# Moving the token stage's tiles under the next stage's first operand, and dropping seven lead steps, in a fused attention forward and backward kernel

## The chip, the cores and the metric

The kernel runs on one core of a Trainium2 chip, as one program. The metric is the device time of a run in microseconds (us); lower is better. The engines are TensorE (PE in the profile, with its weight loads as PEld), VectorE (DVE), ScalarE (ACT), GpSimd (POOL) and SyncE (SP), which here only issues transfers; DMA engines move the data.

## The reference

The reference is the output of a gated mixture of two attention branches, and its gradients with respect to eleven inputs. There are 2048 tokens with 576 channels. Branch A has 32 query heads of 18 channels that share one key and one value head. Branch B goes through the tokens in 64 segments of 32, with 8 memory rows that each segment hands to the next, and has 32 heads of 128 channels.

```
g = sigmoid((x * gate_w).sum(-1))
a = softmax(q k^T / sqrt(18)) v  @ wo          # branch A, all tokens
for s in range(64):                            # branch B
    h = concat([mem, x_s]);  q, k, v = h Wq, h Wk, h Wv
    o = softmax(mask(q k^T / sqrt(128))) v  @ Wo
    mem, out_s = o[:8], o[8:]
out = g * a + (1 - g) * b;   grads = vjp(grad_out)
```

## The kernel before, in words

The program is a row of stages on one core.

1. Preparation and projections, up to about 500 us.
2. The forward weave: the recurrent chain of branch B's segments, with the first pass of branch A between its steps.
3. The token stage, `b_bulk`, about 2040 to 2673 us. It goes through the tokens in 32 chunks (a tile of 128 tokens, half of the heads) of four groups each: scores, softmax, outputs and their gradients for branch B's tokens. The work is a pipeline of short steps over 137 ticks: a group's queries are turned at its own tick and its last step, `st_Qx`, which reads the chunk's keys, comes nine ticks later.
4. The backward weave: the recurrent chain backwards, 64 segments of 14 steps (`b_chain_bwd`), with the second pass of branch A (`a_pass2`, called the sweep: 1024 steps in all) between its steps. `weave` makes one sweep step per chain step. Before the chain it makes `lead` steps without a chain: each of these runs a sweep step, then `early_bwd(i)`, which issues loads, then, from step PRE on, a piece of `lead_dw`, eleven matmuls of two weight gradients of branch A.
5. `b_post`, then `b_dw`: the weight gradients of branch B, with the rest of the sweep, one step each time that the matmuls have streamed WCOLS columns; then `a_final`.

The order on every engine is that of the program, written out by hand. A tile's place in on-chip memory follows from the order of the pools and of the first allocations in them. A stage's tiles overlie those of the stage before it, and a first write waits for the last use of the tiles that lie there. [...]

Names that the steps below touch, with the lines of the profile:

- `x_q`, `x_dO`, `x_k` (L758): 128 x 16 x 128 in bf16, 4,096 B a partition, four buffers of each, rotated by chunk; they are called deep. `x_v` has three buffers, the memory keys and values `x_kmT` and `x_vmT` (L749) two each. `x_kmB` and `x_vmB` (L752), two each of 4,096 B, are masked copies in the pool `xw`, written into their diagonal blocks and zeroed once.
- `x_po<-x_kmB,x_DT` and `x_po<-x_k,x_DT`: the matmuls of `st_Qm` and `st_Qx` (L87 is the line of the helper that makes every matmul). `dqx_dram<-x_dq` (L788): the store of a chunk's query gradients, issued by `flush`; from tick 129 on, `flush` issues on ScalarE's queue.
- `WT` (three tiles of 128 x 32 x 576, 36,864 B a partition): first the operands of `lead_dw`, WT[0] with dq and x (L681, L682), WT[1] with o and da (L684, L686), then the transposed weights of the chain (L1064), two heads of each group of eight at a time, so four loads a tile. `WoT` (L673) is another weight of the chain.
- `r_pj<-WT` and `r_x<-WT`: the matmuls of `lead_dw` (in the chain, `r_pj<-WT,r_dT` are the matmuls `heads` with the weights). `r_kvo` (L712) carries results of `lead_dw` to the output.
- `b_QS` (L2023): the sweep's operand for four steps, loaded by SyncE in the weave and by ScalarE in `b_dw`; `b_S`, `b_dP`, `b_acc`: its matmuls; `b_E` (L2037) the exponential on ScalarE, `b_dS` (L2088) the product on VectorE.

Of the kernel before, what the change touches and what calls it, by code (L numbers as in the profile page):

```python
# [12 lines left out]
BF16 = mybir.dt.bfloat16  # L13
# [3 lines left out]
P = 128  # L17
# [18 lines left out]
KR = 9  # L36
KVT = 11
KV4 = 9
SWEEP = 932
QSW = 800  # L40
WCOLS = 13824
PRE = 7
RIDE = 24


# [6 lines left out]
class Kern:  # L52
# [245 lines left out]
    def weave(self, chain, sweep, lead, extra=(), early=None, pre=None):  # L298
        steps = itertools.count()

        def step():
            i = next(steps)
            next(sweep, None)
            if early is not None:
                early(i)
            if pre is not None and i >= PRE:
                next(pre, None)
# [369 lines left out]
    def early_bwd(self, i):  # L677
        ld = self.nc.sync.dma_start
        v = lambda d: d[:, 0:D].rearrange("(p n) d -> p n d", p=P)
        if i == 0:  # L680
            ld(self.WT[0][:, 16:32, :], v(self.dqtok_dram))  # L681
            ld(self.WT[0][:, 0:16, :], v(self.A_x))  # L682
        if i == 5:
            ld(self.WT[1][:, 0:16, :], v(self.otok_dram))  # L684
        if i == 9:
            ld(self.WT[1][:, 16:32, :], v(self.da_dram))  # L686
        if 13 <= i < 23 and i % 2:
            self.load_WoT((i - 13) // 2)
        for k in range(4):
            if i == 22 + 2 * k:  # L690
                self.load_WT(k)
            if i == 30 + 2 * k:
                self.load_WT(4 + k)
            if i == PRE + 30:
                self.load_WT(8 + k)
# [32 lines left out]
    def b_bulk(self, wp, lp, sp, psum):  # L728
        nc = self.nc
        NTT = self.NTT  # L730
        mx = self.maskX
        mB = {w: [wp.tile([P, 4, 4, E], BF16, name=f"x_{w}mB{i}") for i in range(2)] for w in ("k", "v")}
        mT = {}
        C = {}
# [3 lines left out]
        def load(c, names):  # L738
            if c >= NC:
                return  # L740
            tt, h0 = c // 2, 16 * (c % 2)
            d = C.setdefault(c, {})
            for w in names:
                if w == "mT":
                    if c % 2 == 0:
                        mT[tt] = {}
                        for x in ("k", "v"):
                            mT[tt][x] = lp.tile([P, 4, HB, 8], BF16, name=f"x_{x}mT", bufs=2)
                            nc.sync.dma_start(mT[tt][x][:], self.mTd[x][4 * tt:4 * tt + 4].rearrange("s p h t -> p s h t"))  # L749
                elif w in ("kB", "vB"):  # L750
                    for i in range(4):
                        nc.sync.dma_start(  # L752
                            mB[w[0]][c % 2][32 * i:32 * i + 32, :, i, :],
                            self.mtok[w[0]][tt * 32:(tt + 1) * 32, h0 * P:h0 * P + 2048]
                            .rearrange("r (g i e) -> r g i e", i=4, e=E)[:, :, i, :])
                else:
                    d[w] = lp.tile([P, 16, P], BF16, name=f"x_{w}", bufs=BQ if w in deep else 3)
                    nc.sync.dma_start(d[w][:].rearrange("p h e -> p (h e)"),  # L758
                                      self.xtok[w][tt * P:(tt + 1) * P, h0 * P:h0 * P + 2048])

        after = {4: ("vB",), 5: ("v",), 6: ("mT",), 7: ("q", "dO"), 9: ("k", "kB")}
        deep = ("q", "dO", "k")
        BQ = 4

        def chunk(t, w, shape, bufs):
            d = C[t // 4]
# [229 lines left out]
        for t in range(NG + 9):  # L996
            for n, st in order:
# [4 lines left out]
                for n in done.get(st, ()):  # L1002
                    if t - n >= 0 and (t - n) % 4 == 3:
                        c = (t - n) // 4
                        for w in after[n]:
                            load(c + (BQ if w in deep else 3 if w in ("mT", "v") else 2), (w,))
            if t < 2:
# [6 lines left out]
                else:  # L1014
                    for c in range(3, BQ):
                        load(c, deep)
# [436 lines left out]
    def b_dw(self, sp, wA, wB, wH, psum, sweep):  # L1453
# [6 lines left out]
        def weave(c):  # L1460
            cols[0] += c
            if cols[0] >= WCOLS:
                cols[0] -= WCOLS
                next(sweep, None)
# [746 lines left out]
def build_full(tc, A_x, A_wq, A_wk, A_wv, A_wo, B_mem0, B_Wq, B_Wk, B_Wv, B_Wo, gate_w, grad_out, outs_raw,  # L2211
# [6 lines left out]
    k = Kern(tc, T, A_x, A_wq, A_wk, A_wv, A_wo, B_mem0, B_Wq, B_Wk, B_Wv, B_Wo, gate_w, grad_out, outs=outs)  # L2218
    RIGHT = "right"
    PS = lambda name: tc.tile_pool(name=name, bufs=1, space=bass.MemoryType.PSUM, reuse_waits="tile")  # L2220
    SB = lambda name, side="left": tc.tile_pool(name=name, bufs=1, side=side, reuse_waits="tile")
    with SB("const") as cpool, tc.tile_pool(name="dram", bufs=1, space=bass.MemoryType.DRAM) as dram:
        k.setup_consts(cpool)
        k.setup_A_dram(dram)
        k.setup_B_dram(dram)
        wob = ExitStack()
        bwo = wob.enter_context(SB("bwo", RIGHT))
        dlk = wob.enter_context(SB("dlk", RIGHT))
        with SB("xk") as xk, SB("a1k") as a1k, SB("a1s") as a1s, PS("a1p") as a1p, tc.manual_schedule():
            k.setup_A_consts(cpool)  # L2230
            k.prep(cpool, xk, a1k, a1s, a1p, bwo, lambda: k.setup_B_consts(cpool, a1s))
        items = [("dO", tt) for tt in range(k.NTT)] + [(w, tt) for tt in range(k.XT0) for w in ("k", "v", "q")]
        n0 = k.NTT
        with ExitStack() as man:
            man.enter_context(tc.manual_schedule())
            k.dl_all = dlk.tile([P, k.NTT, 2, NPR, 2], BF16, name="a_dl")
            with SB("bw1") as bw1:
                k.alloc_W(bw1, ("k", "v"))
                prj = ExitStack()
                pds = prj.enter_context(SB("pds", RIGHT))  # L2240
                for n in range(3):
                    k.proj_load(items, n, pds)
                bwt = ExitStack()
                bwt_ = bwt.enter_context(SB("bwt"))
                with PS("wop") as wop:
                    k.make_WoT(bwt_, wop)
                pdp = prj.enter_context(PS("pdp"))

                k.zero512 = pds.tile([64, 512], BF16, name="zero512")
                k.nc.gpsimd.memset(k.zero512[:], 0.0)  # L2250

                def extra(n):
                    if 1 <= n <= 10:
                        k.load_W("kv"[(n - 1) // 5], (n - 1) % 5)
                    if n >= n0 - 4:
                        k.zero_rows(n - n0 + 4)
                k.b_proj(items, 0, n0, pds, pdp, extra)
                bwt.close()
                with SB("bw2") as bw2:
                    k.alloc_W(bw2, ("q",))  # L2260
                    with SB("a2k") as a2k:
                        def extra(n):
                            if n == n0:
                                for kt in range(NKT):
                                    k.load_W("q", kt)
                            elif n == len(items) - 6:
                                k.first_mem(a2k)
                            elif n == len(items) - 4:
                                k.load_A_kv(a2k)
                        k.b_proj(items, n0, len(items), pds, pdp, extra)  # L2270
                        prj.close()
                        with SB("a2s") as a2s, SB("cfs") as cfs, PS("cfp") as cfp, PS("a2p") as a2p:
                            k.weave(k.b_chain_fwd(a2k, cfs, cfp), k.a_pass1(a2k, a2s, a2p, cfp), 2)
            with SB("xw") as xw, SB("xl") as xl, SB("xs") as xs, PS("xp") as xp:
                k.b_bulk(xw, xl, xs, xp)
            wob.close()
            tw = ExitStack()
            twp = tw.enter_context(SB("tw"))
            k.alloc_WT(twp)
            with SB("rw") as rw, SB("rs") as rs, SB("a3k") as a3k, SB("a3s") as a3s, \  # L2280
                    SB("rk") as rk, SB("rv") as rv, SB("rd") as rd, PS("rp") as rp, PS("a3p") as a3p:
                k.alloc_WoT(rw)
                k.weave(k.b_chain_bwd(rs, rd, rv, rk, rp), k.a_pass2(a3k, a3s, a3p, 0, SWEEP, nc.sync, rv, 3), PRE + 29,
                        (), k.early_bwd, k.lead_dw(rv, rp))
            wHs = ExitStack()
            wH = wHs.enter_context(SB("wH", RIGHT))
            with SB("yr", RIGHT) as yr, SB("ys") as ys, PS("yp") as yp:
                k.b_post(ys, yr, yp, wH)
            tw.close()
        with wHs, SB("wA", RIGHT) as wA, SB("wB") as wB, SB("ws") as ws:  # L2290
            with SB("a4s") as a4s, PS("a4p") as a4p, PS("wp") as wp_:
                k.b_dw(ws, wA, wB, wH, wp_, k.a_pass2(a4s, a4s, a4p, SWEEP, 4 * NPR * k.NTT, nc.scalar, a4s, 2))
            with SB("a5s") as a5s, PS("a5p") as a5p, tc.manual_schedule():
                k.a_final(a5s, a5p)
# [76 lines left out]
```

## Time and profile before

| | |
|---|---|
| runs | 5292.52, 5266.23, 5287.8 us; median 5287.8 us |
| profiled execution | 5271.04 us, span 5269.3 us |
| granted TensorE clock, mean | 0.987 |
| forward weave, 500 to 2000 us | PE busy 97% of it |
| token stage, windows 2000 to 2400 and 2400 to 2800 | PE busy 365.80 and 358.22 of 400 us each |
| backward weave, 2800 to 4250 | PE busy 1397.07 of 1450 us, DVE 1175.14, ACT 1138.14 |
| DMA traffic | 959.23 MB, mean 182 GB/s |

A window's row gives start and end, its length, the busy time of PE, weight loads, DVE, ACT and POOL with the number of instructions, then the clock granted to PE as a share of full speed, the mean busy share of the core's 16 DMA engines and the GB/s that they moved. A row of the timeline gives the start, the length, the engine (SPq and ACTq are the queues that SyncE and ScalarE issue transfers from), the line, the operation as out<-in, the count of merged instructions, and in brackets how long the engine sat idle before it and what ended that. A row of the waits gives who waited for whom: us in total, times, longest.

### The profile page before, as it was taken

The numbers are of one execution on the slowest core, as the hardware profiler recorded it, in microseconds if no ns is written. First come the engines' busy times: TensorE is split into PE (matmuls) and PEld (weight loads), VectorE is DVE, ScalarE is ACT, GpSimd is POOL, SyncE is SP. The second block draws the span as 40 slices with busy tenths as digits, with TensorE's granted clock in tenths as the row PEclk, the third lists the DMA queues.
The fourth block names the chain that finished last, engine by engine and source line by source line (L and its number), as shares of the span: only waits on it lengthen the run. The fifth ranks groups of instructions, "written<-read, shape, count | busy, mean of one in ns | idle before, by whom it ended". The sixth has DMA issues, their size and how long they took to land. (4 is left out here: it accounts for less than half of the span.)

```text
span 5269.3 us, 216448 instructions
## 1 busy us (share of the span) xinstructions
PE 5047.8 (96%) x93152; PEld 2783.5 (53%) x93152; DVE 3526.8 (67%) x7041; ACT 3271.2 (62%) x4701; POOL 2167.2 (41%) x4164
## 2 busy tenths in 40 slices
PE   8999999999999998999989999999999999999999
PEld 5444444444444445666654555555555577754445
DVE  4348888888888887666657777878888831333322
ACT  4238888888888886555557777778777732222211
POOL 3015566665655655333323444444444421111113
PEclk9999999999999999999999999999999999999999
DMA  8856766666765455888875787888888778966654
GB/s 273 265 149 138 138 137 143 138 139 137 145 138 127 114 110 177 260 257 256 240 275 161 173 184 173 184 175 184 188 183 182 163 194 212 269 214 188 194 166 138
DMA packets 1070902, 959.23 MB, mean 182 GB/s; under 512 B 618245, under 2 KB 926413, under 8 KB 1059956
## 3 DMA queue, kind: packets, MB, share of 16 engines
q1 hardware_dynamic: 958556, 695.16, 54.6%
q0 software_dynamic: 102032, 240.46, 14.9%
q8 instruction: 728, 11.93, 1.0%
q10 hardware_dynamic: 9352, 9.77, 0.6%
q14 instruction: 234, 1.92, 0.1%
HBM read 518.26 MB, written 375.52 MB: 170 GB/s over the span
## 5 line engine op out<-in xcount | busy, mean ns | idle before, releaser
L2088 DVE TENSOR_TENSOR b_dS<-b_dP,b_E 128x512 bf16<-128x512 f32 x2048 | 1317.3, 685 | 540.0 <-PE b_dP L87 243.5
L1923 DVE TENSOR_TENSOR a_W<-a_dP,a_E 128x512 bf16<-128x512 f32 x2048 | 1313.6, 683 | 225.6 <-issue 105.2
L2037 ACT ACTIVATE b_E<-b_S 128x1024 bf16<-128x1024 f32 x1024 | 1049.3, 1025 | 612.5 <-PE b_dP L87 489.1
L1892 ACT ACTIVATE a_E<-a_S 128x1024 bf16<-128x1024 f32 x1024 | 1050.0, 1025 | 246.1 <-PE a_dP L87 165.3
L87 PE MATMUL a_acc<-a_E,l_VK 128*32 128x512 bf16 x4096 | 593.6, 385 | 5.0
L87 PE MATMUL r_pj<-WT,r_dT 128*32 128x288 bf16 x12288 | 489.4, 289 | 16.8 <-issue 11.2
L87 PE MATMUL w_acc<-w_d,w_h 128*128 128x512 bf16 (+1 forms) x2400 | 484.3, 380 | 0.0
L87 PEld LDWEIGHTS <-b_QS 32*128 32x128 bf16 (+1 forms) x8192 | 240.1, 91 | 440.9 <-issue 398.1
L87 PE MATMUL a_S<-a_QD,l_KV 32*128 32x512 bf16 x2048 | 398.7, 383 | 41.1 <-ACT a_E L1892 38.9
L87 PE MATMUL b_S<-b_KV,b_QS 32*128 32x512 bf16 x2048 | 403.7, 386 | 34.9 <-ACT b_E L2037 22.6
L87 PE MATMUL b_dP<-b_KV,b_QS 32*128 32x512 bf16 x2048 | 405.8, 390 | 6.1 <-issue 4.1
L87 PE MATMUL a_acc<-a_W,l_WK 128*32 128x512 bf16 x2048 | 405.2, 390 | 0.3 <-DVE a_W L1923 0.2
L87 PE MATMUL b_acc<-b_dS,b_QS 128*18 128x512 bf16 x2048 | 399.5, 385 | 0.6 <-issue 0.3
L87 PE MATMUL b_acc<-b_E,b_QS 128*18 128x512 bf16 x2048 | 398.2, 385 | 0.9 <-issue 0.9
L87 PE MATMUL a_dP<-a_QD,l_KV 32*128 32x512 bf16 x2048 | 398.2, 385 | 0.0
L87 PEld LDWEIGHTS <-hm 128*32 128x32 bf16 x7680 | 264.1, 96 | 193.7 <-issue 11.9
L87 PEld LDWEIGHTS <-r_dT 128*32 128x32 bf16 x12288 | 276.9, 96 | 142.6 <-issue 94.9
L87 PEld LDWEIGHTS <-w_h 128*128 128x128 bf16 (+1 forms) x2528 | 215.0, 100 | 245.3 <-issue 16.8
L938 POOL TENSOR_TENSOR x_prod<-x_dOT,x_oT 128x512 bf16<-128x512 bf16 x128 | 148.0, 1156 | 302.6 <-ACT x_oT L935 285.6
L87 PEld LDWEIGHTS <-l_KV 32*128 32x128 bf16 x4096 | 123.9, 91 | 250.8 <-issue 210.4
L87 PE MATMUL x_b<-WoN,x_oT 128*128 128x288 bf16 x1024 | 212.9, 292 | 1.7 <-issue 1.7
L87 PEld LDWEIGHTS <-l_WK 128*32 128x32 bf16 x2048 | 98.9, 93 | 218.5 <-issue 218.5
(473 smaller groups left out, 10153.4 us busy)
## 6 DMA issues: line engine op xcount, KB each, us to landing
b_QS<-qs_dram SPq DMA_DIRECT2D x233, 200.0 KB
dOx_dram<-p_tok SPq DMA_DIRECT2D x16, 1024.0 KB
c_vx<-vx_dram SPq DMA_DIRECT2D x64, 256.0 KB
krow_dram<-c_k POOLq DMA_DIRECT2D x64, 256.0 KB
qrow_dram<-c_q POOLq DMA_DIRECT2D x64, 256.0 KB
vrow_dram<-c_v POOLq DMA_DIRECT2D x64, 256.0 KB
x_q<-qx_dram SPq DMA_DIRECT2D x32, 512.0 KB
x_dO<-dOx_dram SPq DMA_DIRECT2D x32, 512.0 KB
```

The lines of the kernel that those rows point to most:

```text
L87: return self.nc.tensor.matmul(out, lhsT, rhs, start=start, stop=stop, tile_position=tp, skip_group_check=True)
L938: nc.gpsimd.tensor_tensor(out=sc["prod", t][:], in0=sc["dOT", t][:], in1=oT[:], op=ALU.mult)
L1892: nc.scalar.activation(E_[n][:], S.pop(n)[:], ACT.Exp, scale=SCALEA)
L1923: nc.vector.tensor_tensor(out=W_[n][:, i, :], in0=dP[i][:], in1=E_[n][:, i, :], op=ALU.mult)
L2037: nc.scalar.activation(E_[n][:], S.pop(n)[:], ACT.Exp, scale=SCALEA)
L2088: nc.vector.tensor_tensor(out=D_[n][:, i, :], in0=dP[i][:], in1=E_[n][:, i, :], op=ALU.mult)
```

## The change

The deep tiles are no longer rotated buffers of the pool. `b_bulk` lays out four sets of three tiles, x_q, x_dO and x_k of one chunk side by side, as the first tiles of the pool `xl`, and chunk c uses set c % 4. `xl` now comes ahead of `xw`. So the 36,864 B of WT[0] lie under sets 0, 1 and 2, nine tiles of 4,096 B; before, they lay under the four masked tiles, the four x_q and one x_dO. The pools' total is the same.

PRE goes from 7 to 0, and with it `lead` from 36 to 29 steps: `lead_dw` begins in the first step. SWEEP goes from 932 to 925, so that the sweep in the backward weave still ends with the chain; the seven steps are made in `b_dw`, and WCOLS goes from 13824 to 12800. The loads of `early_bwd` get new steps: the WT[1] operands at 1 and 3 (5 and 9 before), WoT from 6 (13), WT[2] from 15 (22), WT[0] again from 22 (30), WT[1] again at 30 (37).

```diff
-SWEEP = 932
+SWEEP = 925
-WCOLS = 13824
-PRE = 7
+WCOLS = 12800
+PRE = 0
...
-        if i == 5:
+        if i == 1:
             ld(self.WT[1][:, 0:16, :], v(self.otok_dram))
-        if i == 9:
+        if i == 3:
             ld(self.WT[1][:, 16:32, :], v(self.da_dram))
-        if 13 <= i < 23 and i % 2:
-            self.load_WoT((i - 13) // 2)
+        if 6 <= i < 16 and i % 2 == 0:
+            self.load_WoT((i - 6) // 2)
         for k in range(4):
+            if i == 15 + 2 * k:
+                self.load_WT(k)
             if i == 22 + 2 * k:
-                self.load_WT(k)
-            if i == 30 + 2 * k:
                 self.load_WT(4 + k)
             if i == PRE + 30:
                 self.load_WT(8 + k)
...
+        deep = ("q", "dO", "k")
+        BQ = 4
+        deepT = [{w: lp.tile([P, 16, P], BF16, name=f"x_{w}{i}") for w in deep} for i in range(BQ)]
...
-                    d[w] = lp.tile([P, 16, P], BF16, name=f"x_{w}", bufs=BQ if w in deep else 3)
+                    d[w] = deepT[c % BQ][w] if w in deep else lp.tile([P, 16, P], BF16, name=f"x_{w}", bufs=3)
...
-            with SB("xw") as xw, SB("xl") as xl, SB("xs") as xs, PS("xp") as xp:
+            with SB("xl") as xl, SB("xw") as xw, SB("xs") as xs, PS("xp") as xp:
                 k.b_bulk(xw, xl, xs, xp)
```

More of the change, by code (lines that the diff above doesn't have):

```diff
@@ L761, in b_bulk @@
         after = {4: ("vB",), 5: ("v",), 6: ("mT",), 7: ("q", "dO"), 9: ("k", "kB")}
-        deep = ("q", "dO", "k")
-        BQ = 4
         def chunk(t, w, shape, bufs):
```

## The prediction

> **What bounds the kernel now.** The page comes first: PE is the engine that is nearly always busy, so a microsecond is gained only where PE waits or runs slowly, and a PE instruction that is added costs its full time wherever PE is full.
>
> ```profile
> span 5269.3 us, 216448 instructions
> PE 5047.8 (96%) x93152; PEld 2783.5 (53%) x93152; DVE 3526.8 (67%) x7041; ACT 3271.2 (62%) x4701; POOL 2167.2 (41%) x4164
> ```
>
> The edits lie at one seam, where the token stage ends and the backward weave begins, so I read windows of 10 us round it (columns: start and end, length, busy time of PE, PEld, DVE, ACT, POOL, then granted clock, DMA share, GB/s).
>
> ```profile
> 2670.00:2680.00 10.00, 3.61 (x65) 1.42 (x57) 2.33 (x6) 4.84 (x8) 0.00 (x0) 0.70 1.00 341
> 2680.00:2690.00 10.00, 6.87 (x50) 1.82 (x48) 7.49 (x12) 5.80 (x6) 0.00 (x0) 0.50 1.00 380
> ```
>
> The hole is 2670 to 2691: PE is busy 3.61 and 6.87 of 10 us at a clock of 0.70 and 0.50, while the DMA engines are full. SyncE's queue says what they carry (start, length, queue, line, what is issued), and its waits say what held it:
>
> ```profile
> 2663.63 5.00 SPq L2023 DMA_DIRECT2D b_QS<-qs_dram  x3
> ...
> 2674.10 0.33 SPq L681 DMA_DIRECT2D WT<-dqtok_dram  x1
> 2674.48 0.44 SPq L682 DMA_DIRECT2D WT<-in_A_x_dram  x1
> ...
> 2685.86 0.62 SPq L684 DMA_DIRECT2D WT<-otok_dram  x1
> ...
> 2696.89 0.43 SPq L686 DMA_DIRECT2D WT<-da_dram  x1
> ```
>
> ```profile
> SPq L681 <- DMA dqx_dram<-x_dq: 5.3, 1, 5.3
> ```
>
> The first operand tile, WT[0], is filled by L681 and L682. PE's timeline shows the end of the stage, the lone sweep steps, and the first matmul that reads WT[0]:
>
> ```profile
> 2665.11 0.40 PE L87 MATMUL x_po<-x_k,x_DT 32*32 32x128 bf16 x16
> ...
> 2672.74 0.38 PE L87 MATMUL x_po<-x_kmB,x_DT 128*128 128x512 bf16 x1 [1.76 <-ACT x_dq L808]
> ...
> 2677.30 0.61 PE L87 MATMUL b_S<-b_KV,b_QS 32*128 32x512 bf16 x2 [3.53 <-ACT b_E L2037]
> ...
> 2690.95 2.82 PE L87 MATMUL r_pj<-WT 128*128 128x288 bf16 x11 [0.74 <-DMA WT<-in_A_x_dram]
> ...
> 2698.50 0.39 PE L87 MATMUL b_S<-b_KV,b_QS 32*128 32x512 bf16 x2
> 2698.82 1.52 PE L87 MATMUL r_pj<-WT 128*128 128x288 bf16 x11
> ...
> 2700.60 0.39 PE L87 MATMUL b_S<-b_KV,b_QS 32*128 32x512 bf16 x2
> ```
>
> The last wait there is a transfer: `r_pj<-WT` starts at 2690.95, released by the A_x load. The lone steps before it fill a wait that DMA sets; they do not set it.
>
> **Part 1, the layout.** Before, WT[0] overlies the mask tiles (mB) and four x_q and one x_dO buffers, so its load needs the last `x_po<-x_kmB` (2672.74 plus 0.38 = 2673.1). After, it overlies sets 0 to 2 of the deep tiles, last read by `x_po<-x_k` of chunk 30 (2665.11 plus 0.40 = 2665.5). SyncE gets to L681 only behind three b_QS issues (2663.63 plus 5.00 = 2668.6). So the most that an earlier load could gain is 2674.1 less 2668.8 = 5.3 us. But the wait row names another releaser: the store of x_dq, whose issue stands on ScalarE's queue:
>
> ```profile
> 2670.88 0.39 ACTq L788 DMA_DIRECT2D dqx_dram<-x_dq  x1
> ```
>
> [...] In the built program of the changed kernel L681 still waits for the completion count of this same store of x_dq, and L682 for that of the x_dS store behind it; only the PE condition has become earlier. Nothing ahead of that issue moves on PE, DVE, ACT or POOL. I take 0 (ends: -5.3 if the lane is free sooner, 0 if not). At the token stage's start the first x_k load no longer waits for the forward weave; PE's waits there name no load, the longest behind the last forward step being one for DVE, so 0:
>
> ```profile
> PE x_tr L92 <- DVE x_qT L836: 1.7, 1, 1.7
> ```
>
> **Part 2, no lone steps.** Seven sweep steps (PRE 7 to 0) leave the lead. With WT[0] landing at 2690.9 as before, the first `r_pj` still starts at 2690.95; PE just stands idle from about 2678. The other 29 lead steps follow at the same 2.10 us (2700.60 less 2698.50). Gain in the lead: 0. The clock costs nothing new: it is 0.50 through the lone steps, and the eleven `r_pj` matmuls take 2.82 us cold against 1.52 us warm already.
>
> **Part 3, where the seven steps go.** SWEEP 932 to 925 puts them into the weight gradients, WCOLS 12800 spacing 95 steps over the same columns (95 x 12800 = 1,216,000; before 88 x 13824 = 1,216,512). There PE is full (677.99 of 680 us), and one step lies bare between two runs of w_acc:
>
> ```profile
> 4480.00:5160.00 680.00, 677.99 (x4615) 358.49 (x4612) 222.81 (x397) 153.51 (x192) 126.72 (x202) 0.99 0.69 208
> ```
>
> ```profile
> 4707.21 0.39 PE L87 MATMUL b_acc<-b_dS,b_QS 128*18 128x512 bf16 x2
> ...
> 4707.86 5.14 PE L87 MATMUL w_acc<-w_d,w_h 128*128 128x512 bf16 x23
> ```
>
> 4707.86 less 4707.21 = 0.65 us; seven make **+4.55 us**. DVE and ACT, which each step also uses, are busy 222.81 and 153.51 us of the 680, so they add nothing; and nothing hides a PE instruction there.
>
> **Part 4, the loads behind.** Relative to the first gradient matmul, the WoT and WT[2] loads keep their places; otok and da (L684, L686) come at steps 1 and 3 and so go out at about 2677 instead of 2685.9 and 2696.9. The last quarter of WT[0]'s second filling (L1064) moves ahead of the chain's own loads. It went out at 2762.00, with the four loads of WT[1]'s second filling from 2764.19 on. That matters in the chain's first segment:
>
> ```profile
> 2762.00 0.57 SPq L1064 DMA_DIRECT2D WT<-st_WT  x1
> ...
> 2764.19 4.42 SPq L1064 DMA_DIRECT2D WT<-st_WT  x4
> ```
>
> ```profile
> 2756.20 1.05 PE L87 MATMUL r_pj<-WoT,dm 128*32 128x512 bf16 x16 [0.22 <-DVE dm L1077]
> ...
> 2777.72 0.67 PE L87 MATMUL r_pj<-WT,r_dT 128*32 128x288 bf16 x16 [1.11 <-DMA WT<-st_WT]
> ...
> 2780.53 1.15 PE L87 MATMUL r_pj<-WT,r_dT 128*32 128x288 bf16 x16 [1.58 <-DMA WT<-st_WT]
> ...
> 2783.53 1.15 PE L87 MATMUL r_pj<-WT,r_dT 128*32 128x288 bf16 x16 [1.86 <-DMA WT<-st_WT]
> ...
> 2787.37 1.90 PE L87 MATMUL r_pj<-WoT,dm 128*32 128x512 bf16 x16
> ```
>
> ```profile
> 2810.91 1.05 PE L87 MATMUL r_pj<-WoT,dm 128*32 128x512 bf16 x16
> ...
> 2833.19 1.05 PE L87 MATMUL r_pj<-WoT,dm 128*32 128x512 bf16 x16
> ```
>
> ```profile
> 2756.00:2760.00 4.00, 2.61 (x41) 1.19 (x45) 3.57 (x8) 1.88 (x3) 1.19 (x2) 1.00 0.50 155
> 2760.00:2764.00 4.00, 3.53 (x132) 1.99 (x121) 2.01 (x4) 2.82 (x5) 1.54 (x4) 1.00 0.35 76
> ...
> 2780.00:2784.00 4.00, 1.61 (x27) 0.99 (x30) 0.36 (x1) 0.05 (x1) 0.00 (x0) 0.50 0.81 268
> ```
>
> The first segment runs from 2756.20 to 2787.37, 31.2 us; the third, 2810.91 to 2833.19, 22.3. Inside it PE waits three times for WT[1]'s second filling: 1.11 + 1.58 + 1.86 = 4.55 us; the clock then falls to 0.50, and sixteen WoT matmuls take 1.90 instead of 1.05 us. I price the slow stretch by the second segment too: 23.5 against 22.3 is 1.2, and the two bursts of sixteen `r_pj` at 1.15 against 0.67 us (the row at 2777.72) with the work up to 2787 about 2; 3.3 in all. So 7.9 us can go. DMA is at 0.50 and 0.35 from 2756 to 2764: the moved quarter (1.18 MB, a fourth of 128 x 36,864 B) fits in before that gap, and the four WT[1] loads then start some 2 to 3 us earlier with 1.18 MB less ahead of them, about 3 us at the 380 GB/s of 2680 to 2690. They would land 5 to 6 us sooner, more than the 4.55. But a lead with its loads packed closer may lag elsewhere, so I take three quarters, **-6 us** (ends -7.9 and 0).
>
> [...] The longest of these three waits is 1.86 us, and the clock still reads 0.50 behind them. [...] The trace shows the drop, and I go by it.
>
> **Part 5, the rest.** Waits of the lead on the stores of r_kvo can move by what the largest now costs, 2.0 us, either way:
>
> ```profile
> 2749.78 0.39 PE L87 MATMUL b_S<-b_KV,b_QS 32*128 32x512 bf16 x2 [2.03 <-ACT b_E L2037]
> ```
>
> In the chain, b_QS loads fall one chain step earlier (36 lead steps before, 29 now, four steps to a load), so SyncE's order of b_QS against r_dT and r_kr changes in each of 64 segments. What PE loses to loads there is small:
>
> ```profile
> PE r_x L87 <- DMA r_kr<-qx_dram: 3.5, 3, 1.9
> PE r_x L87 <- DMA r_kr<-dOx_dram: 1.7, 1, 1.7
> ```
>
> ```profile
> SPq L2023 <- PE b_dP L87: 80.7, 73, 6.6
> SPq L2023 <- PE b_acc L87: 74.1, 24, 6.1
> ```
>
> 5.2 us could go, as much could come; I take 0.
>
> **Sum**: 0 + 0 + 4.55 - 6 + 0 = about -1.5 us. The profiled run took 5271.0 (span 5269.3 and 1.7 around it), so 5269.5 beside it; that run lies 16.8 below the median of the three, 5287.8, which gives **5286**.
>
> **Rivals.**
> *It does what it says* (0.14): the lane is free when SyncE arrives, WT[0] lands 5.3 us sooner and the whole of Part 4 is gained: -5.3 + 4.55 - 7.9 = -8.7, 5279. For it: the PE condition is 7.6 us earlier. Against it: the wait row names the store, and the store stays.
> *Slower: WT[1] crowds WT[0]* (0.14). After, otok and da are queued at 2677, within 3 us of WT[0], on the same queue. If the engines share themselves between the four loads, WT[0] ends with them: 4 x 2.36 MB at the same 380 GB/s is 25 us, so near 2700, and the lead starts about 9 us late: +9 + 4.55 with nothing regained is +13.6, 5301. It decides once the first `r_pj<-WT` starts more than 1.5 us after the 2690.95 of now. Against it: L684 was issued at 2685.86, 5 us before WT[0] was complete, and the three late WT[1] quarters release PE 2.8 and 3.0 us apart (2777.72, 2780.53, 2783.53), so they come one after another. [...]
> *The chain's SyncE order* (0.12): 0.41 us in each of 64 segments would be 26 us, either way (5314 or 5261). Two rows above, 80.7 and 74.1 us that b_QS holds SyncE, show that the queue is often blocked; that PE loses only 5.2 us to r_kr speaks against it. Half of its weight is under 10 us.
> *My forecast* has 0.60.
>
> **How the numbers follow.** Half a per cent, 26 us, is about what a measurement can tell from no change: the three runs alone lie 26.3 apart. Forecast and first two rivals lie inside it; slower by more needs the chain, or crowding with scatter (0.07), faster by more the chain or scatter (0.05); 0.88 remain. The range goes from the lowest run with a gain of 5 (5261) to the highest with a loss of 7.5 (5300); it leaves out the far end of crowding and of the chain.
>
> **What would show it.** L681 some 8.6 us behind the `x_po<-x_k` of chunk 30 (2674.1 less 2665.5), still released by dqx_dram; L684 and L686 within 3 us of it; one idle stretch of PE of about 13 us; `r_pj<-WT` at 2690.9 plus or minus 1; no wait for st_WT in the chain's first segment, which shrinks from 31.2 to about 25; seven more b_S pairs behind the post stage, at 0.65 us each. I am wrong if L681 is issued before 2670, if `r_pj` starts after 2693, or if the segments' mean moves by over 0.1 us.

## The result, and the profile after

The change costs about 15 us. Over 22 runs each, the changed kernel takes 5285.05 us in the median and the kernel before 5269.73; the ratio of their runs is 1.0029 (95% interval 1.0019 to 1.0039). The prediction had 1.5 us less than before. Its 5286 lies close to the 5285 only because the three runs that it started from had a median of 5287.8, 18 above that of the 22.

The page of the profiled run of after (5281.88 us), its head and the line of busy time:

```profile
span 5280.2 us, 216221 instructions
PE 5028.1 (95%) x92971; PEld 2783.5 (53%) x93152; DVE 3527.9 (67%) x7041; ACT 3270.2 (62%) x4701; POOL 2166.8 (41%) x4164
```

**The seam came out as foreseen.** The same windows of 10 us as before (start and end, length, busy PE, PEld, DVE, ACT, POOL, clock, DMA share, GB/s), then SyncE's queue, its wait, and PE's timeline:

```profile
2670.00:2680.00 10.00, 0.61 (x4) 0.10 (x3) 1.29 (x2) 2.63 (x3) 0.00 (x0) 0.50 1.02 381
2680.00:2690.00 10.00, 4.84 (x25) 2.72 (x26) 1.29 (x2) 1.36 (x2) 0.00 (x0) 0.54 1.01 347
```

```profile
2669.50 0.33 SPq L681 DMA_DIRECT2D WT<-dqtok_dram  x1
2669.88 0.43 SPq L682 DMA_DIRECT2D WT<-in_A_x_dram  x1
...
2670.98 0.71 SPq L684 DMA_DIRECT2D WT<-otok_dram  x1
2671.75 15.26 SPq L686 DMA_DIRECT2D WT<-da_dram  x1
```

```profile
SPq L681 <- DMA dqx_dram<-x_dq: 6.8, 1, 6.8
```

```profile
2660.49 0.40 PE L87 MATMUL x_po<-x_k,x_DT 32*32 32x128 bf16 x16
...
2668.71 0.58 PE L87 MATMUL x_po<-x_k,x_DT 32*32 32x128 bf16 x16
...
2685.16 2.82 PE L87 MATMUL r_pj<-WT 128*128 128x288 bf16 x11 [11.87 <-DMA WT<-in_A_x_dram]
```

PE is now idle where it made lone steps: 0.61 of the first 10 us, and the 4.84 of the second are the lead's matmuls from 2685.16 on. L681 comes 8.6 us behind the `x_po<-x_k` of chunk 30 (2660.49 plus 0.40; the row at 2668.71 is the stage's last), as foreseen, and still waits for the store of x_dq, 6.8 us. From the issue of L681 to the first `r_pj<-WT` it takes 2685.16 - 2669.50 = 15.7 us, before 2690.95 - 2674.10 = 16.9: the loads of WT[1], queued close behind, did not delay WT[0]. (In this run all of it lies some 5 us earlier, because the token stage ran faster, so that L681 goes out before 2670, a sign of being wrong in the prediction, though its place behind the stage is as foreseen; that stage's length scatters from 619 to 641 us over the twenty profiles of this study.)

**The stall in the chain's first segment moved.** PE's timeline and SyncE's queue there:

```profile
2749.97 1.05 PE L87 MATMUL r_pj<-WoT,dm 128*32 128x512 bf16 x16 [0.22 <-DVE dm L1078]
...
2758.91 0.21 PE L87 MATMUL r_x<-perm,r_dx 128*128 128x32 bf16 x1 [3.48 <-DMA r_dx<-dmx_dram]
...
2779.61 1.05 PE L87 MATMUL r_pj<-WoT,dm 128*32 128x512 bf16 x16
```

```profile
2754.32 0.33 SPq L1102 DMA_DIRECT2D r_dx<-dmx_dram  x1
...
2758.31 3.45 SPq L1065 DMA_DIRECT2D WT<-st_WT  x4
```

The three waits for `WT<-st_WT` are gone, but `r_x<-perm,r_dx` now waits 3.48 us for a load that SyncE issued only at 2754.32, after it had stood 4.4 us for the landing of a `WT<-st_WT` load (PE waited 0.5 us there before). The segment shrinks from 31.2 to 2779.61 - 2749.97 = 29.6 us, not to 25. The slow stretch moved with the wait. These are windows round the drop of the clock (the third column from the right), first before, then after:

```profile
2776.00:2779.60 3.60, 1.83 (x40) 0.99 (x37) 1.82 (x3) 1.60 (x2) 0.00 (x0) 1.00 1.04 395
2779.80:2783.80 4.00, 1.41 (x24) 0.85 (x27) 0.56 (x1) 0.25 (x1) 0.00 (x0) 0.50 0.84 282
```

```profile
2754.10:2757.40 3.30, 1.33 (x24) 0.52 (x16) 1.29 (x2) 1.87 (x3) 0.66 (x2) 1.00 0.54 142
2757.60:2764.20 6.60, 5.16 (x121) 2.10 (x121) 2.78 (x5) 2.42 (x3) 3.32 (x6) 0.50 0.84 272
```

The clock still falls to 0.50 inside the segment, now within the 3.48 us of the new wait. The rows of before also set a reading of the prediction right: the clock fell there behind the first of the three waits, of 1.11 us, and before the other two had ended, with PE busy 1.83 of the 3.60 us ahead of the drop.

**Up to there after is ahead; it loses later.** The weight gradients, by the rows of `w_acc` (count, duration in ns, first and last start) and of the first matmul of the last stage. First the kernel before, then after:

```profile
L87 PE MATMUL w_acc<-w_d,w_h x2400: 379/379/405, 4677.0 to 5222.0; 128*128 128x512 bf16 x148, 128*64 128x512 bf16 x37
L87 PE MATMUL w_acc<-w_h,w_d x1280: 283/286/448, 4486.2 to 4675.7; 128*128 128x288 bf16 x183
```

```profile
L92 PE MATMUL f_ptr<-identB,w_d x80: 216/219/230, 5222.3 to 5254.3; 128*128 128x128 bf16 x80
```

```profile
L87 PE MATMUL w_acc<-w_d,w_h x2340: 379/379/404, 4681.7 to 5230.4; 128*128 128x512 bf16 x154, 128*64 128x512 bf16 x41
L87 PE MATMUL w_acc<-w_h,w_d x1280: 286/286/448, 4482.6 to 4680.4; 128*128 128x288 bf16 x183
```

```profile
L92 PE MATMUL f_ptr<-identB,w_d x80: 216/219/314, 5230.7 to 5265.2; 128*128 128x128 bf16 x80
```

The first phase (matmuls `w_acc<-w_h,w_d`) took 4677.0 - 4486.2 = 190.9 us and now takes 199.1; the second took 5222.3 - 4677.0 = 545.3 and now takes 549.0. Together 11.9 us, where the prediction had 4.55. And in the chain PE stands idle longer. These are the waits from 2800 to 4250 that the profile calls issue, time in which PE waits for nothing that it shows (us in total, times, longest), before and after:

```profile
PE r_pj L87 <- issue: 11.5, 14, 2.5
...
PE b_dP L87 <- issue: 4.1, 2, 2.1
...
PE r_x L87 <- issue: 3.5, 5, 2.0
...
PE b_acc L87 <- issue: 1.2, 2, 0.9
```

```profile
PE r_pj L87 <- issue: 15.8, 20, 3.2
...
PE r_x L87 <- issue: 7.5, 6, 2.7
PE b_dP L87 <- issue: 4.7, 3, 2.5
PE b_acc L87 <- issue: 3.4, 3, 1.7
PE b_S L87 <- issue: 1.5, 2, 0.9
```

They add up to 20.3 us before and 32.9 after. One of them in the timeline of after, in the middle of a run of equal matmuls, ahead of which the profile shows nothing that they wait for:

```profile
3685.49 1.04 PE L87 MATMUL r_pj<-WT,r_dT 128*32 128x288 bf16 x27
3689.75 0.66 PE L87 MATMUL r_pj<-WT,r_dT 128*32 128x288 bf16 x5 [3.22 <-issue]
```

### The profile page after: what moved, and what is told of

Its sections match the earlier page's. It is cut to its first block, busy times and chain, and to the rows that moved or that the text cites. A ratio compares the mean times of both kernels' runs of the same rounds, so it can differ in the third digit from the quotient of the medians.

```text
span 5280.2 us, 216221 instructions
## 1 busy us (share of the span) xinstructions
PE 5028.1 (95%) x92971; PEld 2783.5 (53%) x93152; DVE 3527.9 (67%) x7041; ACT 3270.2 (62%) x4701; POOL 2166.8 (41%) x4164
## 3 DMA queue, kind: packets, MB, share of 16 engines
q8 instruction: 728, 11.93, 1.0%
## 5 line engine op out<-in xcount | busy, mean ns | idle before, releaser
L87 PE MATMUL b_S<-b_KV,b_QS 32*128 32x512 bf16 x2048 | 403.1, 386 | 30.4 <-ACT b_E L2038 17.8
```

What stands on the lines that cost most here:

```text
L87: return self.nc.tensor.matmul(out, lhsT, rhs, start=start, stop=stop, tile_position=tp, skip_group_check=True)
```

## The experiments

Two theories: **A**, the loss sits in the chain, because with 29 lead steps instead of 36 the b_QS loads of the sweep fall on other chain steps; **B**, it sits in the weight gradients alone. The rival **C**: the layout costs. The chain step of a load is counted from the chain's start, modulo four: 36 lead steps and a load at n % 4 == 1 give step 1 (the kernel before), 29 give step 0. A segment has 14 steps, so within a segment the loads lie two steps further in every other one.

All kernels in one table. *Ratio* is to the kernel before, with its 95% interval (0.0010 is 5.3 us). *Step* is the chain step of the loads; w: the load waits for the `b_acc` of the same sweep step, which frees its buffer; n: the buffer is free a step or more earlier. The stages are from each kernel's one profile, by first starts of matmuls: *seam* from the token stage's end to the chain's second segment, *chain* from there to its end, *dw1* and *dw2* the two phases of the weight gradients. *Late* is the issue idle in the last sixth of every other segment (the second, fourth and so on), summed; after has 2.0 in the other segments. Each chain is one profile: before and e1 run the same chain and differ by 13.8 us in it, after, f2 and f4 by 4.0.

| kernel | ratio | step | seam | chain | late | dw1 | dw2 |
|---|---|---|---|---|---|---|---|
| before | 1 | 1 w | 113.9 | 1465.2 | 5.7 | 190.9 | 545.3 |
| after | 1.0029 (1.0019 to 1.0039) | 0 w | 110.3 | 1471.4 | 21.5 | 199.1 | 549.0 |
| e1 layout | 0.9994 (0.9983 to 1.0006) | 1 w | 114.1 | 1451.4 | 2.0 | 193.1 | 545.3 |
| e2 loads | 1.0004 (0.9994 to 1.0014) | 1 w | 110.6 | 1446.7 | 1.4 | 191.6 | 545.3 |
| e3 steps | 1.0038 (1.0024 to 1.0052) | 0 w | 112.1 | 1478.6 | 18.4 | 199.1 | 549.0 |
| e4 three back | 1.0005 (0.9994 to 1.0016) | 1 w | 110.6 | 1459.5 | 4.3 | 192.0 | 547.7 |
| f1 chain later | 1.0006 (0.9993 to 1.0018) | 1 n | 109.5 | 1456.8 | 10.1 | 195.7 | 549.0 |
| f2 dw later | 1.0028 (1.0013 to 1.0044) | 0 w | 111.4 | 1467.9 | 17.8 | 192.6 | 549.0 |
| f3 both later | 1.0004 (0.9990 to 1.0018) | 1 n | 109.9 | 1460.2 | 16.9 | 193.6 | 549.0 |
| f4 z_src first | 1.0046 (1.0029 to 1.0064) | 0 w | 113.4 | 1467.4 | 16.7 | 192.7 | 549.0 |
| g1 no b_QS | 0.9958 (0.9944 to 0.9971) | none | 113.0 | 1421.4 | 0.0 | 200.0 | 549.0 |
| g2 | 0.9982 (0.9967 to 0.9996) | 2 n | 114.1 | 1438.4 | 2.6 | 191.4 | 545.3 |
| g3 | 1.0001 (0.9986 to 1.0015) | 3 n | 113.5 | 1458.6 | 6.5 | 190.7 | 545.3 |
| g4 | 0.9993 (0.9980 to 1.0006) | 2 n | 108.0 | 1442.1 | 4.3 | 199.6 | 549.0 |
| h1 | 0.9973 (0.9958 to 0.9987) | 2 n | 108.8 | 1444.6 | 7.0 | 191.4 | 545.3 |
| h2 | 1.0018 (1.0001 to 1.0034) | 0 n | 114.0 | 1447.0 | 5.7 | 192.0 | 545.3 |
| h3 | 0.9990 (0.9975 to 1.0005) | 2 n | 113.8 | 1443.7 | 1.9 | 192.9 | 549.0 |
| h4 ACT queue | 1.0144 (1.0123 to 1.0166) | 0 w | 110.6 | 1514.9 | 0.0 | 198.9 | 549.0 |
| i1 fifth buffer | 0.9993 (0.9977 to 1.0009) | 0 n | 106.2 | 1471.0 | 6.9 | 193.9 | 549.0 |
| i2 four back | 1.0016 (0.9999 to 1.0033) | 0 w | 111.1 | 1464.7 | 14.4 | 197.3 | 547.3 |

### The change taken apart

**e1, the layout alone** in the kernel before: the `deepT` and `xl` lines of the diff.

> The kernel before with the new layout alone (deep tiles set by set, their pool first); all steps and loads as before. Theory A (the loss sits in the chain, where seven fewer lead steps shift the b_QS loads against r_dT and r_kr) and theory B (the loss sits in the weight gradients: seven added steps and a later opening) both expect no difference: within 3 us of the kernel before, with L681 still released by the store of x_dq. Theory C (the layout itself costs) expects most of the 15 us, +10 or more.

0.9994, and L681 still waits for `dqx_dram<-x_dq` (7.9 us). The layout costs and gains nothing; C is out.

**e2, the packed loads alone:**

```
-        if i == 5:
+        if i == 1:
             ld(self.WT[1][:, 0:16, :], v(self.otok_dram))
-        if i == 9:
+        if i == 3:
             ld(self.WT[1][:, 16:32, :], v(self.da_dram))
...
-            if i == 30 + 2 * k:
+            if i == 29 + 2 * k:
                 self.load_WT(4 + k)
```

> The kernel before with the packed loads alone: otok at step 1, da at step 3, and the second filling of WT[1] one step earlier; seven lone steps and the old layout stay. If the stall in the chain's first segment is all that changes, -3 to -6 us and no wait of r_pj for st_WT. Theories A and B expect that. If the packed loads cost (crowding, a later lead), +5 or more, and the first r_pj on WT starts after 2693.

Its waits of PE from 2660 to 2810 have no `WT<-st_WT` any more, but the same new one as after:

```profile
PE r_x L87 <- DMA r_dx<-dmx_dram: 4.2, 1, 4.2
```

The seam is 3.3 us shorter than before (113.9 to 110.6); the times (1.0004, 0.9994 to 1.0014) do not show a gain of that size, nor exclude one of 3.

**e3, the seven steps alone** (PRE 0, SWEEP 925, WCOLS 12800, old layout, loads shifted by seven steps, that of o by five):

> The kernel before with the seven steps moved alone (PRE 0, SWEEP 925, WCOLS 12800), loads at the same distance from the first gradient matmul as before, old layout. Theory A expects +11 to +15: 4.55 for the steps and some 0.1 us in each of 64 segments. Theory B expects +12 to +15 as well, but with the segments' mean where it was (23.3 us without the first) and the weight gradients 10 to 12 us longer. By the prediction's own sum it is +4.5.

1.0038, which is 20 us: this edit alone makes the whole loss. The lead gains little from it: PE waits 11.2 us where it made lone steps, and the seam is 112.1 against 113.9.

```profile
PE r_pj L87 <- DMA WT<-in_A_x_dram: 11.2, 1, 11.2
```

**e4, after with three lone steps back** (PRE 3, SWEEP 928, WCOLS 13184):

> The changed kernel with three lone steps put back (PRE 3, SWEEP 928, WCOLS 13184, loads shifted by three steps): 32 lead steps, so the b_QS loads fall in the chain where they fell with 36. Theory A expects the chain's 6 to 9 us back and two us of steps: +4 to +6 against the kernel before. Theory B expects only three steps' worth back, 2 us: +12 to +13.

1.0005: three steps bring back nearly all of it, where three times 0.65 would be 2 us. B in the form on record, three steps' worth, can't explain that; A does. But 928 also starts the sweep of the weight gradients on another step of a page, and their first phase falls from 199.1 to 192.0 us, so e4 alone does not tell the chain from the opening of the weight gradients. The next runs do.

### Chain or weight gradients

`a_pass2` gets a parameter ph, which is 1 so far:

```
-                if n % 4 == 1:
+                if n % 4 == ph:
                     load(n // 4 + 3)
```

**f1**: after, ph 2 in the chain only. **f2**: ph 2 in the weight gradients only. **f3**: both.

> The changed kernel, with the b_QS load of the chain's sweep issued at the second step of a page instead of the first (the sweep in the weight gradients unchanged): with 29 lead steps the loads then fall on the chain step they fell on with 36. Theory A (the chain's order costs) expects 5 to 10 us back: +5 to +10 against the kernel before, with the segments' mean at 23.0 to 23.2 instead of 23.4 to 23.5 and the first phase of the weight gradients still 199 us. Theory B (only the weight gradients cost) expects no change from the changed kernel: +12 to +20.

> The changed kernel, with the same later load in the weight gradients' sweep alone: its first load of a page then goes out at the second of the six opening steps, as before the change. If that load's place makes the opening slow (transposes behind it on lanes, z_src late), the first phase falls from 199.1 to about 192.5 us and the stall of z_pt goes: +6 to +10 against the kernel before. If it doesn't, the phase stays at 199 and the time at +12 to +20.

> The changed kernel with both later loads. If both places cost, only the seven steps are left (+4.55) less what the lead gains (about 3): +1 to +3 against the kernel before. If neither does, +12 to +20.

f1 (1.0006) is as fast as before: with the loads one step later in the chain, and nothing else undone, the loss is gone. That is A, and the chain's share of it by the times is about 12 us (1.0029 less 1.0006, give or take some 8 by the two intervals), by the profiles 1470.0 (mean of the five kernels with step 0 w on SyncE's queue) less 1456.6 (mean of the six with step 1) = 13.4. In the same five and six chains the issue idle is 29.4 against 18.2 us, and PE is busy for 1412 against 1406 us with the same matmuls. In f2 the first phase falls to 192.6 as expected, but its time (1.0028) is no better than after's; an interval of plus or minus 8 us leaves room for the 5 that the phase lost. f3 equals f1.

What f2's profile shows is the opening of the weight gradients. Their sweep makes six steps first. With 925 it starts on the step that loads a page, with 932 one step ahead of it. SyncE's queue (start, length) and PE's timeline in after:

```profile
4479.64 11.98 SPq L1478 DMA_TRANSPOSE w_d<-oh_dram  x4
4491.73 1.01 SPq L618 DMA_DIRECT2D z_src<-dTm_dram  x2
```

```profile
4497.77 0.40 PE L92 MATMUL z_pt<-identB,z_v 128*128 128x128 bf16 x4 [1.76 <-DVE z_v L629]
4499.52 0.61 PE L92 MATMUL z_pt<-identB,z_v 128*128 128x128 bf16 x4 [1.35 <-POOL z_v L629]
```

The transposes of `w_d` take 11.98 us to issue for four; the loads of `z_src` go out behind them at 4491.73, 9.1 us after the first `w_acc`; PE waits 1.76 and 1.35 us for `z_v`, and from 4498.4 to 4505.1 its clock is 0.50. In f2:

```profile
4472.17 7.59 SPq L1478 DMA_TRANSPOSE w_d<-oh_dram  x4
4479.87 1.06 SPq L618 DMA_DIRECT2D z_src<-dTm_dram  x2
```

```profile
4490.36 0.61 PE L92 MATMUL z_pt<-identB,z_v 128*128 128x128 bf16 x8
```

The four take 7.59 us, `z_src` goes out 2.3 us after the first `w_acc` (4477.6), and PE does not wait. The windows of the whole first phase, after and then f2, show the rest of the difference in PE's busy time: nearly the same matmuls take 3.4 us longer (195.80 against 192.41) at the lower mean clock (0.97 against 0.99).

```profile
4482.60:4681.70 199.10, 195.80 (x1673) 141.64 (x1673) 67.36 (x123) 49.53 (x69) 32.05 (x49) 0.97 0.89 244
```

```profile
4477.60:4670.20 192.60, 192.41 (x1674) 140.51 (x1673) 67.41 (x123) 49.51 (x69) 32.08 (x49) 0.99 0.87 244
```

Over the twenty kernels the first phase has 193.9 to 200.0 us, mean 198.0, in the eight that start on a loading step with the transposes in their old place, and 190.7 to 193.6 in the others. In f2, f3 and h3, which have as many steps as after, it is 193.0: the opening costs 5.0 us by the profiles. `z_src` goes out 6.8 us later than in f2. 4.4 of them are the issue of the four transposes ahead of it (11.98 against 7.59), 2.4 that of the four before those (18.04 against 15.62). In the earlier four of after there lies a wait of 5.9 us for a load that ScalarE issued, `b_KV`, which f2 does not have:

```profile
SPq L1478 <- DMA b_KV<-kv_dram: 5.9, 1, 5.9
```

But f2 waits there too, 3.5 us for `w_d<-ox_dram` and 2.2 for `b_QS<-qs_dram`. Why the later four take longer to issue is not shown, and no run shows the lanes that the expectation of f2 names.

**f4**: after, the two `z_src` loads ahead of the first transposes.

```
+            mem = self.mem_tok(0, sp, psum)
+            next(mem)
             nxt = load(0)
...
-                if k % 4 == 0 and k < 12:
+                if k % 4 == 0 and 0 < k < 12:
```

> The changed kernel with the two z_src loads ahead of the first transposes on SyncE's queue. The stall of z_pt (3.1 us) should go and the clock should warm sooner: first phase 193 to 196 us instead of 199.1, +8 to +14 against the kernel before. If the z_src loads do not set that wait, nothing moves.

The first phase falls to 192.7, as it should, but the stretch before it, from the post stage's start to the first `w_acc`, grows from 226.8 to 234.4: the first `z_src` load now holds SyncE's queue for 24.3 us, until `y_pdx` is done, and the transposes behind it are late instead. 1.0046. The wait was moved, not removed.

### Which property of the load

**g1**: after, without the chain's b_QS loads (the first eleven pages, 0 to 10, still come).

```
-            if 4 * c < hi:
+            if c > 10 and lo == 0:
+                Q[c] = Q[c - 4]
+            elif 4 * c < hi:
```

> The changed kernel without the b_QS loads of the chain: from the eleventh page on, the sweep in the chain works on the last four pages again (so its dk and dv sums are left out of the reference's values; every instruction of PE, DVE and ACT stays). Theory A, in the form that the b_QS loads crowd what PE's late waits in a segment hang on, expects the chain from 1471 to 1450 or less and the idle time that the profile calls issue there from some 30 to 10 us or less: 0 or below against the kernel before. If the chain's excess has nothing to do with these loads, it stays at +12 to +20.

0.9958, the chain at 1421.4, and of 32.9 us of issue idle in the chain 3.0 are left:

```profile
PE r_pj L87 <- issue: 2.3, 6, 0.9
...
PE b_acc L87 <- issue: 0.5, 2, 0.3
...
PE r_x L87 <- issue: 0.2, 1, 0.2
```

Nothing else of PE's work changed, so these loads do bring most of that idle about. They cost more than idle. These are the windows of the chain from its second segment on, after and then g1:

```profile
2779.60:4251.00 1471.40, 1410.60 (x33709) 772.86 (x33705) 1187.45 (x2016) 1149.27 (x1564) 639.87 (x1124) 0.99 0.77 174
```

```profile
2789.40:4210.80 1421.40, 1393.54 (x33709) 769.69 (x33705) 1187.23 (x2016) 1146.85 (x1564) 641.94 (x1124) 1.00 0.64 148
```

Of the 50.0 us between the two chains, 29.9 are issue idle, and 17.1 are the same 33,709 matmuls, busy longer at a clock of 0.99 instead of 1.00.

**g2** and **g3**: the kernel before with ph 2 and 3 in the chain. **g4**: after with ph 3.

> The kernel before with the chain's b_QS loads one step later (chain steps 2, 6, 10 ... instead of 1, 5, 9 ...). If the chain step of the load decides, this is a third value between or beyond those of the steps 0 (+15 with 4.6 for the steps) and 1 (0): -5 to +12, and the same chain time as the changed kernel with loads at the third step of a page. If only the place within the page decides (behind the b_acc that frees the buffer, or a step later), it is -5 to 0, like the first repaired kernel.

> The kernel before with the chain's b_QS loads two steps later (chain steps 3, 7, 11 ...). If the chain step decides, a fourth value of the same curve, -5 to +12. If only the place within the page decides, -5 to 0.

> The changed kernel with the chain's b_QS loads two steps later: with 29 lead steps they fall on chain steps 2, 6, 10 ... If the chain step decides, its chain is as long as that of the kernel before with the loads one step later, within 8 us, and the whole differs by the seven steps less the lead's gain, +2. If only the place within the page decides, its chain is at 1450 to 1460, as in the first repaired kernel.

g2 is faster than the kernel before (0.9982). g4, with the same chain step and 29 lead steps, has its chain within 4 us of g2's (1442.1 and 1438.4); g3 is at 1458.6. So the chain step decides more than the place within the page: step 2 is best in the profiles (mean of the four kernels 1442.2), steps 1 and 3 are some 15 us behind.

**h2**: the kernel before with its loads at step 0, a page asked for one step earlier, so that its buffer is free.

```
-                if n % 4 == 1:
+                if lo == 0 and n > 0 and n % 4 == 0:
+                    load(n // 4 + 2)
+                if lo > 0 and n % 4 == 1:
                     load(n // 4 + 3)
```

**i1**: after with five b_QS buffers in the chain (`bufs=5 if lo == 0 else 4`). **i2**: after with four lone steps back (PRE 4, SWEEP 929, WCOLS 13312): step 0 again, with the wait.

> The kernel before, with only the chain's b_QS loads moved to chain steps 0, 4, 8 ... (a page is asked for one step earlier; 36 lead steps, seven lone ones, old layout and loads). If the chain step of the load alone makes the loss, its chain is as long as in the four kernels with loads at step 0 (1467 to 1479 us from the second segment on, against 1447 to 1465) with some 18 us of issue idle in the last sixth of the odd segments: +6 to +15 against the kernel before. If it needs the shorter lead or the changed counts of transfers, it stays within 4 us of it.

> The changed kernel with a fifth b_QS buffer in the chain: the loads stay at chain steps 0, 4, 8 ..., but no longer wait for the b_acc of the same step that frees their buffer. If the loss comes from that wait at that step (SyncE held, r_dT and r_q behind it late), the chain falls from some 1471 to 1447 to 1460 and the whole to +4 or less against the kernel before. If the step alone makes it, or the shorter lead, it stays at 1467 or more, +12 to +20.

> The changed kernel with four lone steps put back (PRE 4, SWEEP 929, WCOLS 13312): 33 lead steps, so the b_QS loads fall on chain steps 0, 4, 8 ... and wait for the b_acc of the same step, as with 29. One more step is back than in the run with three, so by the count of steps it should be as fast or faster (0 to +2). If step and wait make the loss, its chain is 1467 us or more and it is slower than the run with three steps back: +7 to +15 against the kernel before.

i2 undoes more of the change than e4, and is not faster but, by its middle, slower (1.0016 against 1.0005), with 14.4 us of late idle against 4.3; the intervals overlap. Part of the difference lies in the weight gradients, since 929 is a loading step again and 928 is not: their first phase is 197.3 in i2 and 192.0 in e4. i1 is at 0.9993, 19 us below after, though only a buffer was added; but its one profile shows a chain of 1471.0. h2 is the reverse: a chain of 1447.0 in the profile and 1.0018 by its times. Both have little late idle (5.7 and 6.9; the five with step 0 w have 14.4 to 21.5). That points to step 0 with the wait as the place of the late idle, but does not settle it: f1 and f3, at step 1 and without the wait, have 10.1 and 16.9 of it and no loss. Whether step 0 without the wait costs a few us is open too: the times and the profiles of these two kernels contradict each other.

**h4**: after with the chain's sweep loads on ScalarE's queue (`nc.sync` to `nc.scalar`).

> The changed kernel with the chain's b_QS loads issued by ScalarE at the same step, not by SyncE. If the loss comes from SyncE's order (r_dx, r_q and r_dT behind a b_QS issue), the chain falls to 1455 or less and the whole to +8 or less against the kernel before. If it comes from the transfers themselves crowding others at that time, whoever issues them, the chain stays at 1467 or more and the whole at +12 to +20.

```profile
PE b_S L87 <- ACT b_E L2038: 66.6, 69, 3.5
```

`b_S` waits 66.6 us for the exponential on ScalarE, which now issues the loads too. The author's reading is that ScalarE stands at a load until `b_acc` frees the buffer, as SyncE does in after (28 waits for `b_acc` from 2800 to 4250, 54.8 us); this is not shown for ScalarE. The new wait hides the question that the run was to answer; whether SyncE's order or the transfers themselves make the idle stays open.

### The better version

**h1**: the kernel before with e2's loads and ph 2 in the chain. **h3**: after with ph 3 in the chain and ph 2 in the weight gradients.

> The kernel before with the packed loads and the chain's b_QS loads at chain steps 2, 6, 10 ...; seven lone steps stay in the lead. Gains found so far: 10 (loads at step 2) and 3 (packed loads, by the stages). -13 expected against the kernel before, -8 to -18.

> The changed kernel with the chain's loads at chain steps 2, 6, 10 ... and the later first load in the weight gradients. What is left of the change is the seven steps (+5) and the lead (-3.5), beside the 10 to 15 us that the chain step gains: -8 expected against the kernel before, -3 to -14; some 5 us slower than the kernel that keeps the lone steps.

h1 is the fastest kernel that does all the work: 0.9973 (0.9958 to 0.9987), 14 us below the kernel before. It adds the packed loads to g2 (0.9982); the intervals don't show that these gain anything more. h3, repaired as far as it goes but without the lone steps, is at 0.9990, by the middles some 9 us behind h1; the intervals overlap.

## Why the prediction was wrong, step by step

- **Part 1, the layout: right.** 0 was taken, the reason being that the load waits for a store; e1 measures 0.9994 and shows that wait. No run shows the lane that the ends of this part and the first rival speak of; what the runs show in its place is L681 waiting for the store of x_dq: 5.3 us before, 6.8 in after, 7.9 in e1.
- **Part 2, no lone steps: right.** 0 in the lead; e3's seam is 1.8 us shorter, and in after it takes 15.7 us from L681 to `r_pj`, 16.9 before.
- **Part 3, the seven steps: right in size, but it priced only the steps.** 4.55 us was the sum. f2, f3 and h3, whose opening is repaired, have 742.0 us of weight gradients in the mean, the seven kernels with 932 (before, e1, e2, g2, g3, h1, h2) 736.9: 5.1. What it left out is where the sweep resumes. SWEEP 925 starts it on a loading step, and the opening then takes 5.0 us more by the profiles. The times don't show these 5: f2 is 0.5 us below after, f3 1 us below f1, each give or take some 10.
- **Part 4, the loads behind: the direction right, the size not.** -6 was taken. The three waits went, and in their place stood the next transfer, r_dx, with 3.48 us, and within that wait the clock fell to 0.50 again, so that the slow stretch, 3.3 of the 7.9 us that were priced, stayed in part. The seam is 3.4 us shorter: 110.5 in the mean of the fourteen kernels with packed loads, 113.9 of the five with the old loads and lone steps. The prediction had asked what is late next and had answered only "the lead may lag elsewhere".
- **Part 5, the chain: the step that failed.** "I take 0" for the order of b_QS against r_dT and r_kr. It is 12 to 13 us, 0.2 us in each of 64 segments; the rival "The chain's SyncE order" had it, at 0.41 us and a chance of 0.12. The rows chosen as evidence against it were PE's waits for `r_kr`, 5.2 us. They were the wrong rows to weigh: the loss shows as issue idle, 20.3 us before, which the prediction neither quoted nor priced, and as a lower clock with it: the five times that the clock falls to 0.50 in after's chain (from 2779.60 on) come within such a wait, of 1.38 to 3.22 us, or up to 1.5 us behind its end. Its own sign of being wrong, a segments' mean that moves by over 0.1 us, came: 0.21 us by the means of the five and the six kernels (13.4 over 63 segments). That the place of the loads against the chain makes the loss is shown (f1, g1, g2); by which link a load holds PE up stays open.
- **The sum.** -3.4 + 5.1 + 5.0 + 13 = 19.7 by stages, where 15.3 (10 to 21) was measured for after and 20 for e3. With the scatter of the chains in the 13, and the 5.0 seen in the profiles alone, it could as well have missed by several us.

## What to carry to other kernels

A count of steps that is taken out of a lead also shifts everything that happens every n-th step behind it: ask for each periodic load on which step of the repeated body it will now fall, at the start of the loop and where a split loop resumes. Idle time that a profile puts down to nothing is still a term of the sum, and one with a cause; take a suspected load away altogether once (g1) to see how much hangs on it, and then move it (g2). Where waits in a row are removed, the next transfer in the queue is the one to price.

## What the runs showed of the hardware that was not expected

The idle that the profile calls issue falls behind the landing of packets of one DMA queue, which the trace calls instruction (packets, MB, share of 16 engines):

```profile
q8 instruction: 728, 11.93, 1.0%
```

Its 11.93 MB are 64 bytes for each of PE's 186,123 matmuls and weight loads; from these two counts the author takes the queue to be PE's. In after's chain a packet lands every 5.6 us. Of the 191 issue waits of over 0.8 us in the chains of the twenty profiles, 176 end 1.2 to 1.9 us behind the landing of such a packet; by chance it would be about one in eight. The packets take no longer when they run (1.1 us in the middle, in after as in before); if PE waits for them, they would have to start late, which is not shown. Of the 268 packets that land in after's chain, its first segment included, 16 are followed by an issue wait of over 0.8 us. All the issue idle there comes to 32.9 us. That a b_QS load at the wrong step makes such a packet late is argued from the coincidence and from g1 (3.0 us left), not shown by a run that touches these packets alone.
